# First stage of a fused attention and MLP layer: x transposed a unit ahead, V products in banks of their own, V weights summed by ScalarE, two weight pieces fetched ahead

## The chip, the cores and the metric

The kernel runs on one core of a Trainium2 chip. The metric is the device time of one execution in microseconds. Three runs of the kernel before gave a median of 1518.57 us (1517.03 to 1524.56). The profile is of a separate execution, which took 1515.59 us.

A core has five engines, each with a queue that it works through in order: TensorE (PE; its weight loads are listed as PEld), VectorE (DVE), ScalarE (ACT), GpSimd (POOL) and SyncE (SP), which issues all DMAs of this kernel. Engines wait for each other by semaphores. TensorE's clock is granted by a throttle: 1.00 is full speed.

## The reference

The input x has 2048 rows of 512. It is normalized over its columns; the result feeds an attention of 32 heads of 16 columns and, in parallel, an MLP of width 1792. Both are added to x:

```python
def _A_ref(x, wqkv, wo):                 # D = 512, H = 32, Dh = 16
    q, k, v = split_heads(x @ wqkv)
    p = softmax(einsum("bhqd,bhkd->bhqk", q, k) * Dh ** -0.5)
    return merge_heads(einsum("bhqk,bhkd->bhqd", p, v)) @ wo
def _B_ref(x, w1, b1, w2, b2):           # F = 1792, tanh gelu
    return gelu(x @ w1 + b1) @ w2 + b2
xn = _layernorm(x)
return x + _A_ref(xn, A_wqkv, A_wo) + _B_ref(xn, B_w1, B_b1, B_w2, B_b2)
```

`split_heads` and `merge_heads` stand for the reshapes and transposes of the original.

## The kernel before

**Number format.** Operands are scaled by powers of two and split into a high and a low float16 part, and a product is the sum of three (high-high, high-low, low-high). So each weight piece has first to be read once for its largest magnitude or the sum of its magnitudes; from that come the scales.

**Units.** Attention is worked off four heads and 512 queries at a time, in 16 units per such tile, 512 units in all. Of a unit, `s_half` makes the scores [q, k] that only serve the row maxima: 4 quarter products into one of three S banks, and one VectorE reduce (`mt`, L259); four of them to a unit. `s_end` turns the 16 units' maxima into one column (`mneg`, L270). 19 units later (LEAD), `e_half` makes the transposed scores (pT), ScalarE exponentiates them (`pe`), and `v_half` multiplies with V. What is left of TensorE goes to a fill: first V products, then projections of further heads, MLP, output projection. A fill group is 12 to 42 products.

**The first stage** (from L897) is what has to be there before units can start. x arrives in 16 row tiles of 128 (`load_x`); four of them are a block. `stats` normalizes a block, `transpose_x` turns one of its four column chunks with four TensorE transposes into a bank, copies it out as the high part (L816) and subtracts for the low part, on VectorE (L822) for chunks 0 and 2 and by a ScalarE copy `pf` and GpSimd (L819, L820) for chunks 1 and 3. `project` makes the query or key rows of four heads for one block (12 products of 128x512), writes them to DRAM (`stg`, L503, L504), and `stacks` reads them back in the order that the scores need (L403). Block 0 goes through first; then, for blocks 1, 2 and 3, a projection of keys and one of queries, and four first-tile units `tile_and_unit` (scores and maxima only), with 3 V products after each pair of score halves. Block 2 is transposed after its predecessor's four units, block 3 between units 4 to 7. `prep_v` measures the two halves of the V weights on VectorE (`am_v`, L742), makes their scale and splits them (L144, L145).

**Weight pieces.** 18 pieces of 512 KB (`chunk`, `fetch`, tile `wch`, three buffers, which the two V halves use first) are read in this stage for their magnitudes alone: seven of w1, seven of w2 and two of wo by a ScalarE sum (L850), and last two of the Q/K weights of further heads by VectorE (L742). `measure` hands them out, one or two after each unit; `fetch` issues the DMA of one piece ahead of the one in use. All these DMAs stand in SP's one queue with the x loads and the stacks. After the stage, `prepare` (L994 to L1000) reduces the sums and makes the scales; `rest` fills with the remaining V groups and the projections.

**What sets the order.** In the first stage TensorE's order is the program's (`manual_schedule`); the other engines' instructions are ordered by a list scheduler with its own costs, except those marked `keep_in_program_order`. From unit 16 on every queue is in program order. PSUM has eight banks: three S, three T, one D, one V. `vbank` goes round a list of tags (`free`): before, T, D, T, V, T for transposes, projections and V products alike. `NV` V groups of 12 products are made in the first stage, the others by the fill; units 16 to 18 take 36 products in bursts (`LFILL`).

The end is `last_one`: the last head group's output is normalized, transposed, split (L385 to L391) and multiplied with the last rows of wo; final adds are VectorE's (L1156).

Of the kernel before, what the change touches and what calls it, by code (L numbers as in the profile page):

```python
# [9 lines left out]
F32 = mybir.dt.float32  # L10
# [8 lines left out]
P = 128  # L19
S = 2048  # L20
D = 512
# [21 lines left out]
GELU_C = 0.7978845608028654  # L43
# [8 lines left out]
def layer_kernel(ctx: ExitStack, tc: tile.TileContext, x, wqkv, wo, w1, b1, w2, b2, out):  # L52
# [492 lines left out]
    def run(gen):  # L545
        for _ in gen:
            pass
# [169 lines left out]
    with ExitStack() as st1:  # L717
# [23 lines left out]
        def absmax(dst, v):  # L741
            nc.vector.tensor_reduce(dst, v, axis=AX.XY if len(v.shape) == 3 else AX.X, op=ALU.max,  # L742
                                    apply_absolute_value=True)
            given("dve", 600)
# [5 lines left out]
        every = [w1v[:, :, i * W:(i + 1) * W] for i in range(7)]  # L750
        every = every + [w2v[:, 2 * i:2 * i + 2, :] for i in range(7)] + [wov[:, 0:2, :], wov[:, 2:4, :]]
        wqk = wqkv[:, 0:2 * D].rearrange("(c p) (w n) -> p w c n", p=P, w=2)
        every = every + [wqk[:, w, :, W:2 * W] for w in range(2)] + every
        NM = 18
        amx = work.tile([P, 16], F32, name="amx")
        am_all = work.tile([P, 16], F32, name="am_all")
        fac1, inv1 = [], []

        def fetch(k):
            while len(loads) <= min(k + 1, NM + 15):  # L760
                loads.append(chunk(every[len(loads)]))
            return loads[k]

# [43 lines left out]
        def vbank():  # L807
            turn[0] += 1
            return banks(free[turn[0] % len(free)])
# [17 lines left out]
        def prep_v():  # L827
            am = work.tile([P, 3], F32, name="am_v")
            for i in range(2):
                absmax(am[:, i:i + 1], wvf[i])  # L830
                yield
            nc.vector.tensor_tensor(am[:, 2:3], am[:, 0:1], am[:, 1:2], op=ALU.max)
            box = []
            yield from scales(am[:, 2:3], 1, sbank, box)
            inv, fac = box
            fac_v.append(fac)
            for i in range(2):
                cs = slice(i * W, (i + 1) * W)
                split(wvh[0][:, :, cs], wvh[1][:, :, cs], wvf[i], inv[:, 0:1])

        def some(gen, n):
            for _ in range(n):
                next(gen, None)

        def measure():

            for n in range(16):
                v = fetch(n)
                dst = am_all[:, n:n + 1] if n < 7 else amx[:, n:n + 1]
                pin(nc.scalar.activation(v, v, AF.Abs, scale=1.0 / SPREAD, accum_out=dst))  # L850
                yield
            for w in range(2):
                v = fetch(16 + w)
                for m in (2, 3):
                    absmax(am_all[:, 8 + 2 * m + w:9 + 2 * m + w], v[:, :, (m - 2) * P:(m - 1) * P])
                yield
            for w in range(2):
                absmax(am_all[:, 10 + w:11 + w], wfs[1][w])
                yield

        ms = measure()

        def v_tiles():
            for t in range(NV):
                yield from whole(v_group(t, wvh, lambda: (vbank(), None)))

        vs = v_tiles()

        def tile_and_unit(t):

            for k in range(2):
                s_half(t, 2 * k)
                s_half(t, 2 * k + 1)
                some(vs, NV * 12 // 32)
            s_end(t)

        def weave(*gens):
# [39 lines left out]
            run(whole(project(0, w, 0, ready_w[0], lambda: (vbank(), None), True)))  # L917
        for w in (1, 0):
            stacks(0, w, [0])
        with tc.manual_schedule(engines={mybir.EngineType.PE}):  # L920
            free[:] = ["T", "D", "T", "V", "T"]
            for c in range(NC):
                transpose_x(1, c)
            some(pv, 2)
            for sb in range(1, NQB):
                ln = stats(sb + 1) if sb < 3 else iter(())
                for w in (1, 0):
                    pj = whole(project(0, w, sb, ready_w[0], lambda: (vbank(), None)))
                    for n in range(3):
                        some(pj, 4)  # L930
                        some(pv, 1)
                        if sb == 2:
                            some(ln, 3)
                    run(pj)
                run(pv)
                for w in (1, 0):
                    stacks(0, w, [sb])
                if sb == 1:
                    wfs.append(load_qk(1))
                if sb == 1:  # L940
                    clear(1)
                for j in range(4):
                    tile_and_unit(4 * sb - 4 + j)
                    some(ms, MEASURE[sb])
                    if sb == 1:
                        some(ln, 4)
                    elif sb == 2:
                        transpose_x(3, j)
                if sb == 1:
                    for c in range(NC):  # L950
                        transpose_x(2, c)
            for j in range(4):
                tile_and_unit(NT - 4 + j)
                some(ms, MEASURE[0])
            run(vs)
            run(ms)
        nc.sync.dma_start(b1_s, b1.rearrange("(f p) -> p f", p=P))
# [324 lines left out]
```

## Time and profile before

| | before |
|---|---|
| median of three runs | 1518.57 us |
| profiled execution | 1515.59 us |
| its span, first to last instruction | 1513.8 us |
| busy PE, DVE, ACT, POOL | 1476.7, 1384.8, 1257.5, 661.8 us |
| mean granted clock of TensorE | 0.993 |
| first transposed scores (pT), where the main stage begins | 117.60 us |
| last product with V of the main stage | about 1498.6 us |

A row of the order in time has the start, the length, the engine, the line, the operation, what it writes and reads, the count of merged instructions, and in brackets the idle time before it and who ended it. An instruction may be listed with its pipeline time, so neighbours overlap. Rows with SPq are DMA issues, and their length includes waits of the queue.

### The profile page before, as it was taken

To read this page: it belongs to the slowest core of one execution; us is meant where nothing else is said; L and a number is where in the kernel's file an instruction comes from. 1 tells how busy PE (TensorE), PEld (TensorE's weight loads), DVE (VectorE), ACT (ScalarE), POOL (GpSimd) and SP (SyncE) were. 2 spreads that over 40 slices of the span, in tenths; PEclk is the share of its full clock that TensorE was granted. 3 is DMA by queue.
4 is the path that set the end of the run, shared out by engine and by line. 5 is a ranking of instruction groups with operands and counts; after the bars stand their busy time and mean duration, and the time that the engine had idled before them with its cause. 6 is when DMAs were issued, how large, how long until landed. Compare 5 with 4: busy or idle time off the path is not lost.

```text
span 1513.8 us, 87872 instructions
## 1 busy us (share of the span) xinstructions
PE 1476.7 (98%) x39986; PEld 818.1 (54%) x39986; DVE 1384.8 (91%) x2317; ACT 1257.5 (83%) x2348; POOL 661.8 (44%) x686
## 2 busy tenths in 40 slices
PE   7889999999999999999999999999999999999998
PEld 3335555555555555555555555555555555555554
DVE  8679889999999999999999999999999999999933
ACT  5538878888899888899988889998888998888875
POOL 4101879522777511277831137772115787111110
PEclk9999999999999999999999999999999999999999
DMA  7451667314322311131111211132002210121432
GB/s 243 144 179 47 187 197 243 118 56 133 90 65 75 95 49 34 36 81 53 40 46 46 61 46 44 37 82 59 28 24 63 74 38 22 50 60 25 138 98 93
DMA packets 114413, 124.80 MB, mean 82 GB/s; under 512 B 24700, under 2 KB 86012, under 8 KB 114040
## 3 DMA queue, kind: packets, MB, share of 16 engines
q1 hardware_dynamic: 114040, 119.19, 26.6%
q8 instruction: 312, 5.11, 1.5%
q14 instruction: 61, 0.50, 0.1%
HBM read 81.66 MB, written 37.34 MB: 79 GB/s over the span
## 4 chain that ended last, share of the span: by engine, by line
PE 82%; DVE 9%; DMA 3%; issue 2%; SPq 1%; ACT 1%; POOL 1%; DVEq 0%; ACTq 0%; POOLq 0%
PE pV L168 24%; PE pD L168 22%; PE pT L168 17%; PE pS L168 17%; DVE mt L259 7%; PE pT L437 1%; DMA qk_d<-stg 1%; DMA wch<-in_B_w_dram 1%; DMA m_d<-mhl 1%; PE pD L437 1%; DMA wch<-in_A_wqkv_dram 0%; DMA wch<-in_A_wo_dram 0%; DMA xs<-in_A_x_dram 0%; ACT wch L850 0%; SPq L367 0%
## 5 line engine op out<-in xcount | busy, mean ns | idle before, releaser
L259 DVE TENSOR_REDUCE mt<-pS 128x1 f32<-128x512 f32 x2048 | 1306.9, 684 | 52.2 <-PE pS L168 31.7
L304 ACT ACTIVATE pe<-pT 128x512 f32<-128x512 f32 x2048 | 1111.7, 599 | 178.7 <-PE pT L168 74.6
L168 PE MATMUL pV<-pe,vv 64*32 64x512 f32 x8192 | 1075.2, 595 | 0.3 <-issue 0.2
L168 PE MATMUL pT<-qst,kst 64*32 64x512 f16 x8192 | 712.9, 377 | 6.4 <-DMA qst<-m_d 3.4
L168 PE MATMUL pS<-kst,qst 62*32 62x512 f16 x8192 | 622.4, 378 | 3.5 <-DVE mt L259 1.1
L168 PEld LDWEIGHTS <-qst 62*32 62x32 f16 x8192 | 280.5, 92 | 224.1 <-issue 56.9
L168 PEld LDWEIGHTS <-kst 64*32 64x32 f16 x8192 | 279.4, 91 | 175.1 <-issue 75.8
L168 PE MATMUL pD<-xb,wc 64*32 64x512 f16 x5376 | 360.8, 377 | 0.0
L168 PE MATMUL pD<-w_s,g 64*32 64x512 f16 x5376 | 359.2, 377 | 0.0
L168 PEld LDWEIGHTS pV<-pe,vv 64*32 64x32 f32 x8192 | 182.3, 105 | 90.2 <-issue 2.7
L168 PE MATMUL pD<-xt,wqk_h 64*32 64x512 f16 x2304 | 152.6, 378 | 1.0 <-issue 1.0
L168 PEld LDWEIGHTS <-wc 64*32 64x32 f16 x5376 | 116.8, 91 | 43.2 <-issue 1.1
L168 PEld LDWEIGHTS <-g 64*32 64x32 f16 x5376 | 113.1, 91 | 44.0
L360 POOL TENSOR_TENSOR osb<-osb,rb 128x512 f32<-128x512 f32 x31 | 39.8, 1284 | 203.8 <-DMA rb<-den_d 180.6
L1124 POOL TENSOR_TENSOR xa<-xa,yt 128x512 f32<-128x512 f32 x16 | 20.4, 1278 | 230.0 <-ACT yt L1122 200.8
L1079 POOL TENSOR_TENSOR t<-hh 128x512 f32<-128x512 f32 x56 | 58.2, 1040 | 69.4 <-ACT hh L1099 68.6
L1074 POOL TENSOR_TENSOR t<-t,hh 128x512 f32<-128x512 f32 x56 | 71.8, 1282 | 4.7
L1081 POOL TENSOR_TENSOR t<-t,hh 128x512 f32<-128x512 f32 x56 | 71.8, 1282 | 4.7
L1076 POOL TENSOR_TENSOR g<-t,g 128x512 f16<-128x512 f32 x56 | 65.1, 1163 | 4.7
L168 PEld LDWEIGHTS <-wqk_h 64*32 64x32 f16 x2304 | 53.3, 92 | 20.9 <-issue 3.4
L1073 POOL TENSOR_SCALAR t<-t,gs 128x512 f32<-128x512 f32 x56 | 38.8, 692 | 48.7 <-ACT t L1068 48.7
L168 PE MATMUL pD<-wo_s,oc 64*32 64x512 f16 x828 | 54.5, 378 | 0.0
(151 smaller groups left out, 863.7 us busy)
## 6 DMA issues: line engine op xcount, KB each, us to landing
wch<-in_B_w_dram SPq DMA_DIRECT2D x28, 512.0 KB
wc<-w_d SPq DMA_DIRECT2D x56, 256.0 KB
qk_d<-stg SPq DMA_DIRECT2D x32, 256.0 KB
rb<-den_d SPq DMA_DIRECT2D x124, 64.0 KB
w_d<-wsp SPq DMA_DIRECT2D x28, 256.0 KB
kst<-qk_d SPq DMA_DIRECT2D x128, 48.0 KB
qst<-qk_d SPq DMA_DIRECT2D x128, 48.0 KB
xs<-in_A_x_dram SPq DMA_DIRECT2D x16, 256.0 KB
```

The costliest lines, as they stand in the source:

```text
L168: p = nc.tensor.matmul(*args, **kw)
L259: nc.vector.reduce_max(mt_of[t][:, n, qt, kb:kb + 1], s, axis=AX.X)
L304: nc.scalar.activation(pe, st, AF.Exp, scale=scale_of[g // 2])
L360: pooled((1280, lambda: nc.gpsimd.tensor_tensor(osb, osb, rb, op=ALU.mult)), (620, lambda: nc.gpsimd.tensor_scalar(ot[:, 0], osb, 1.0, 0.0 ...
L437: nc.tensor.matmul(self.bank, lhs, rhs, start=start, stop=self.last and self.over())
L1073: pooled((690, lambda: nc.gpsimd.tensor_scalar(t1, t1, 1.0, gs[:, 1:2], op0=ALU.add, op1=ALU.mult)), (1280, lambda: nc.gpsimd.tensor_tenso ...
L1074: (1280, lambda: nc.gpsimd.tensor_tensor(t1, t1, hh, op=ALU.mult)),
L1076: (1160, lambda: nc.gpsimd.tensor_tensor(g[:, 1, f, :], t1, g[:, 0, f, :], op=ALU.subtract)),
L1079: pooled((1040, lambda: nc.gpsimd.tensor_tensor(t1, hh, hh, op=ALU.mult)), (620, lambda: nc.gpsimd.tensor_scalar(t1, t1, 1.0, 1.0 / GELU_A ...
L1081: (1280, lambda: nc.gpsimd.tensor_tensor(t1, t1, hh, op=ALU.mult)),
L1124: add = lambda: nc.gpsimd.tensor_tensor(xa, xa, yt, op=ALU.add)
```

## The change

- `transpose_x` of block 2 moves into unit 3 and behind it, that of block 3 into units 5 and 6, as an argument of `tile_and_unit`. Behind unit 3, 12 V products follow the transposes, ahead of projection 2.
- `free` is T alone from block 1 on, for transposes and projections; V groups take the D and the V bank in turn.
- The two V halves are summed by ScalarE, in program order, into a scratch tile.
- The two Q/K pieces become the first measured instead of the last, with the two maxima of the next heads' weights; `fetch` issues two pieces ahead in the first stage.
- Pieces are measured one after each unit and one after projections 2 and 3.
- `NV` is 8 instead of 9: one V group more is left to the fill.

Lines of the changed file are one lower than before up to L753 (`MEASURE` is gone).

```diff
-MEASURE = (2, 1, 1, 1)
-NV = 9
+NV = 8
...
-        every = every + [wqk[:, w, :, W:2 * W] for w in range(2)] + every
+        every = [wqk[:, w, :, W:2 * W] for w in range(2)] + every + every
...
-            while len(loads) <= min(k + 1, NM + 15):
+            while len(loads) <= min(k + (1 if pos[0] else 2), NM + 15):
...
         def prep_v():
-                absmax(am[:, i:i + 1], wvf[i])
+                junk = ph.tile([P, 4 * W], F32, name="wch", bufs=3)
+                tc.keep_in_program_order(nc.scalar.activation(junk.rearrange("p (a b) -> p a b", b=W), wvf[i], AF.Abs,
+                                                              scale=1.0 / SPREAD, accum_out=am[:, i:i + 1]))
...
         def measure():
+            for w in range(2):
+                v = fetch(w)
+                for m in (2, 3):
+                    absmax(am_all[:, 8 + 2 * m + w:9 + 2 * m + w], v[:, :, (m - 2) * P:(m - 1) * P])
+                absmax(am_all[:, 10 + w:11 + w], wfs[1][w])
+                yield
             for n in range(16):
-                v = fetch(n)
+                v = fetch(2 + n)
...
-                yield from whole(v_group(t, wvh, lambda: (vbank(), None)))
+                yield from whole(v_group(t, wvh, lambda t=t: (banks("DV"[t % 2]), None)))
...
-        def tile_and_unit(t):
+        def tile_and_unit(t, *chunks):
             for k in range(2):
                 s_half(t, 2 * k)
                 s_half(t, 2 * k + 1)
                 some(vs, NV * 12 // 32)
+                if chunks and chunks[k] is not None:
+                    transpose_x(t // 4 + 2, chunks[k])
...
+        some(pv, 2)
         with tc.manual_schedule(engines={mybir.EngineType.PE}):
-            free[:] = ["T", "D", "T", "V", "T"]
+            free[:] = ["T"]
+            some(pv, 1)
             for c in range(NC):
                 transpose_x(1, c)
...
+            for j in range(4):
+                tile_and_unit(j, [None, None, None, 0][j], [None, None, None, 1][j])
+                some(ms, 1)
+                some(ln, 8)
+            for sb in (2, 3):
+                if sb == 2:
+                    transpose_x(2, 2)
+                    some(vs, 3)
+                    transpose_x(2, 3)
+                    some(vs, 9)
+                    ln = stats(3)
...
+                some(ms, 1)
                 for j in range(4):
-                    tile_and_unit(4 * sb - 4 + j)
-                    some(ms, MEASURE[sb])
+                    t = 4 * sb - 4 + j
+                    if sb == 2:
+                        tile_and_unit(t, [None, 0, 2, None][j], [None, 1, 3, None][j])
+                    else:
+                        tile_and_unit(t)
+                    some(ms, 1)
```

More of the change, by code (lines that the diff above doesn't have):

```diff
@@ L930, in layer_kernel @@
                         some(pj, 4)
[L931 to L933 removed]
+                        some(ln, 3)
                     run(pj)
[L935 removed]
+                run(ln)
                 for w in (1, 0):
                     stacks(0, w, [sb])
[L938 to L941, printed above, removed]
+                some(ms, 1)
                 for j in range(4):
[L943 to L951 removed]
+                    t = 4 * sb - 4 + j
[4 more added lines that the diff above has]
+                    some(ms, 1)
             for j in range(4):
                 tile_and_unit(NT - 4 + j)
[L954 removed]
+                some(ms, 1)
             run(vs)
```

23 lines of the change are left out of this document (12 added, 11 removed).

## The prediction

> **What bounds the kernel now.** I read the shares of the page first, then busy time by stretches, then the order in time of each engine, and last the end.
>
> ```profile
> span 1513.8 us, 87872 instructions
> PE 1476.7 (98%) x39986; PEld 818.1 (54%) x39986; DVE 1384.8 (91%) x2317; ACT 1257.5 (83%) x2348; POOL 661.8 (44%) x686
> ```
>
> TensorE is busy for 98% of the span; 37 us are idle. Stretches of busy time (columns: length, busy of PE, PEld, DVE, ACT, POOL with instruction counts, granted clock, DMA share, GB/s) show where:
>
> ```profile
> 21.20:33.20 12.00, 9.64 (x43) 5.28 (x43) 10.65 (x34) 8.23 (x14) 2.31 (x2) 0.86 0.66 181
> 33.20:45.80 12.60, 11.41 (x105) 5.04 (x105) 12.60 (x20) 6.18 (x12) 1.54 (x1) 1.00 0.76 224
> 45.80:57.70 11.90, 8.30 (x24) 2.80 (x24) 5.56 (x18) 9.60 (x19) 2.31 (x2) 0.71 0.26 84
> 57.70:68.70 11.00, 11.00 (x105) 5.07 (x105) 10.10 (x17) 4.08 (x8) 2.31 (x2) 1.00 0.56 163
> 68.70:77.60 8.90, 5.67 (x34) 2.31 (x32) 1.63 (x3) 6.20 (x12) 1.15 (x1) 1.00 0.48 149
> 77.60:99.50 21.90, 21.90 (x198) 7.70 (x198) 19.22 (x32) 10.21 (x18) 1.16 (x1) 1.00 0.71 227
> 99.50:105.00 5.50, 1.03 (x12) 0.29 (x4) 2.80 (x6) 1.35 (x4) 0.00 (x0) 0.86 0.74 232
> 105.00:117.60 12.60, 12.49 (x83) 4.31 (x84) 8.25 (x18) 1.42 (x3) 0.00 (x0) 0.79 0.34 96
> 117.60:1498.60 1381.00, 1369.97 (x39225) 773.74 (x39224) 1289.43 (x2116) 1202.26 (x2249) 639.08 (x633) 1.00 0.25 72
> ```
>
> These are: x block 1 transposed and projected; tiles 0 to 3; x block 2 and its projection; tiles 4 to 7; projection 3; tiles 8 to 15 and a ninth V group; a wait; units 16 to 18, up to the first transposed scores (pT) at 117.60; the main stage; then the end. The change edits the first eight. What ended the waits (start, length, and in brackets the idle time before and its releaser):
>
> ```profile
> 23.43 1.16 PE L815 MATMUL pT<-ident,xs 128*128 128x128 f32 x4 [2.23 <-DVE xs L802]
> 34.98 9.65 DVE L259 TENSOR_REDUCE mt<-pS 128x1 f32<-128x512 f32 x16
> 45.54 1.06 ACT L850 ACTIVATE wch<-wch 128x1024 f32<-128x1024 f32 x1 [5.65 <-DMA wch<-in_B_w_dram]
> 50.95 6.82 PE L437 MATMUL pT<-xt,wqk_h 128*128 128x512 f16 x20 [1.14 <-POOL xt L820]
> 74.43 0.59 PE L437 MATMUL pT<-xt,wqk_h 128*128 128x512 f16 x2 [2.38 <-POOL xt L820]
> 96.46 2.75 PE L437 MATMUL pV<-wvh,xt 128*128 128x512 f16 x12
> 105.03 0.43 PE L277 MATMUL pS<-ident,mneg 64*32 64x64 f32 x4 [4.51 <-DVE mneg L270]
> 103.48 1.28 DVE L742 TENSOR_REDUCE am_all<-wch 128x1 f32<-128x512 f32 x2 [0.83 <-DMA wch<-in_A_wqkv_dram]
> ```
>
> At 45.54 ScalarE had stood 5.65 us before a weight piece; x's copies for projection 2 are queued behind it, so that projection ends at 57.7. A group of 12 products takes 2.75, so 24 take 5.5 at full clock. Between 99.5 and 105 VectorE waits for the last two pieces ahead of the row maxima (mneg). Tiles are VectorE's: 16 reduces in 9.65 us, 0.603 each, four to a tile.
>
> **The change, part by part.** I follow the changed kernel's own order on each queue and write times on the clock of the profile.
>
> *V sums on ScalarE, projection 1.* The rows that carry this part:
>
> ```profile
> 18.04 1.18 DVE L742 TENSOR_REDUCE am_v<-wch 128x1 f32<-128x1024 f32 x1
> 21.23 0.60 ACT L509 ACTIVATE stg<-pS 128x512 f16<-128x512 f32 x1 [0.46 <-PE pS L437]
> 22.87 1.34 ACT L800 ACTIVATE xs<-xs,sd 128x512 f32<-128x512 f32 x2 [1.04 <-DVE sd L794]
> 96.92 1.06 ACT L850 ACTIVATE wch<-wch 128x1024 f32<-128x1024 f32 x1
> 49.74 1.15 POOL L820 TENSOR_TENSOR xt<-pf,xt 128x512 f16<-128x512 f32 x1 [13.67 <-ACT pf L819]
> ```
>
> VectorE loses two reduces of a V half, 1.2 us each. ScalarE gains two sums like the one at 96.92, 1.15 each with the read-out. They stand behind the second projection copy (21.23, done by 21.8) and around two x scalings (1.34): 21.8 to 22.9, the scalings, 24.2 to 25.4. TensorE's order now puts the transpose of these sums ahead of x block 1, so block 1 starts at 25.9, not 23.43. All its transposes take the three T banks; the fourth waits for a copy (28.9). Piece 0, now a Q/K piece, is issued behind eight transfers of block 0, about 27.5, and VectorE stands before it, ahead of the scale of V and of x's third low part. The flight of a piece:
>
> ```profile
> 33.89 0.38 SPq L736 DMA_DIRECT2D wch<-in_B_w_dram  x1
> 38.19 1.06 ACT L850 ACTIVATE wch<-wch 128x1024 f32<-128x1024 f32 x1 [0.73 <-DMA wch<-in_B_w_dram]
> 98.10 5.36 DMA wch<-in_A_wqkv_dram
> 41.11 1.49 SPq L736 DMA_DIRECT2D wch<-in_B_w_dram  x3
> 83.94 7.03 SPq L736 DMA_DIRECT2D wch<-in_B_w_dram  x5
> ```
>
> 4.3 us alone, 5.4 among three. I take 4.3, since little else flies then: landing 31.8, two reduces 1.3, x's low part 33.8. The array is cold then, by these rows:
>
> ```profile
> 25.00:28.50 3.50, 3.50 (x15) 0.51 0.32 91
> 103.20:110.20 7.00, 5.09 (x27) 0.52 0.10 33
> ```
>
> After 2.2 us idle the clock was 0.51 in 25 to 28.5; after 4.5 us idle it was 0.52 until 5.2 us past the restart at 105.03. The changed kernel idles 4.7 us and then works in bits; a product at half clock takes 0.43. From 33.4 on it is busy: the clock is back near 38, 11 or so products at 0.43 and the rest at 0.23 end projection 1 at 39. Tile 0 starts at 39.5, not 34.98: **+4.5**. Bounds: +1.5 (piece 0 early, full clock, the later start alone) to +6 (a flight of 5.4).
>
> The Trainium skill, "TensorE: Matmul & The Clock Gate", section "What's actually happening", says that the array is halved after an idle window of about 3.4 us and freed after a busy one of that length. It speaks against this change, since the new gap of 4.7 us is longer than that and the old one was not; the trace halved the clock after 2.2 us already. By the rule the clock would be back at 36.8 instead of 38 and the sum 0.6 us lower.
>
> *x a unit ahead, projection 2.* Tiles 0 to 3 carry 16 reduces (9.65), two of piece 1 (1.3) and one low part (0.6): 39.5 to 51. Block 2's first two chunks are transposed in tile 3, the rest beside 12 V products that stood elsewhere (below). Pieces 3 to 5 go out behind block 1's stacks at 46 (41.11 before, later by the delay of projection 1) and land from 50.5. On ScalarE, piece 3 stands ahead of x's chunks 2 and 3: 50.5 to 51.6, copies to 53.2, GpSimd's low part 54.4. The V products cover TensorE until 53. Projection 2 goes on from there with about 0.2 us of wait and ends at **58.1**, 0.4 behind the 57.7 of before: the 6.4 us that the old one lost to ScalarE's wait and the cold clock pay for the late start. If the cover fails (piece 3 lands 3 us later), it costs these 3 and some 2.3 of cold clock.
>
> *Projection 3.* Block 3 is transposed in tiles 5 and 6, and no measured piece stands before its copies any more. Tiles 4 to 7 take 11.0 as before, the projection 5.5 instead of 8.9. It ends at 74.6: **3.0 ahead**. What is late next: ScalarE measures pieces 6, 7, 8 and 10 around the two evictions, which puts the query eviction at 78 and its stacks and pieces 11 to 17, queued behind on SP, at 84.0, no earlier than the 83.94 of before.
>
> *Tiles 8 to 15.* 32 reduces:
>
> ```profile
> 77.99 19.22 DVE L259 TENSOR_REDUCE mt<-pS 128x1 f32<-128x512 f32 x32 [1.55 <-PE pS L168]
> 98.73 1.06 ACT L850 ACTIVATE wch<-wch 128x1024 f32<-128x1024 f32 x1 [0.65 <-DMA wch<-in_A_wo_dram]
> 107.72 0.14 DVE L997 TENSOR_REDUCE am_all<-amx 128x1 f32<-128x2 f32 x1
> 111.50 0.41 PE L168 MATMUL pS<-kst,qst 62*32 62x512 f16 x8
> 117.60 0.60 PE L168 MATMUL pT<-qst,kst 64*32 64x512 f16 x8
> ```
>
> They end at 94.2. The ninth V group (2.75 at 96.46) isn't there, nor the wait for two pieces: mneg is ready at 95, **10 ahead** of 105.03.
>
> *Units 16 to 18.* Seven pieces are left behind SP's 83.94, as many as ScalarE measured then in the old kernel; its last began at 98.73, so the last ends near 99.9. VectorE's three small reduces for the scales stand there, ahead of the reduces of unit 17. TensorE has banks and V products until about 99.5. From the fourth S half of unit 17 to pT it needed 117.60 - 111.50 = 6.1; restarting at 101 it has pT at **107.1, 10.5 ahead**. With no wait (12.6 at a clock of 0.79 is 10.0 at full clock) it would be 105.0.
>
> *Own banks, pieces two ahead.* Tiles show no wait of TensorE for a bank, and SP's order, not the look-ahead, releases the pieces: nothing, from 0 to 1 us of gain where V products no longer share T.
>
> *Eight V groups.* The ninth moves to the main stage's fill, 12 products in half arrays. No unit is longer for it; the order of the end shows the remainder: 60 and 12 quarter-column products and six whole ones between the last transposes and the last output group, where 8 and 12 stood, and nine final adds on VectorE instead of six:
>
> ```profile
> 1505.90 0.68 DVE L391 TENSOR_TENSOR ot<-pS,ot 64x512 f16<-64x512 f32 x1 [1.46 <-ACT ot L390]
> 1506.51 0.73 DVE L1156 SCALAR_TENSOR_TENSOR ac<-pS,gs,ac 128x512 f32<-128x512 f32 x1
> 1507.16 3.37 DVE L1156 SCALAR_TENSOR_TENSOR ac<-pD,gs,ac 128x512 f32<-128x512 f32 x5
> ```
>
> Five adds take 3.37, so three more are **+2.0** after 1505.90; bounds 0 (they run while VectorE waits) and 2.75 (a whole group).
>
> *Sum:* -10.5 + 2.0 = -8.5 us. The profiled execution took 1515.59 us (span 1513.8 and 1.8 around it): 1507.1. The median of the runs shown, 1518.57, lies 3.0 above it, so I forecast 1510.1.
>
> **The rivals.** (a) ScalarE still holds x back: piece 3 lands at 53.5, projection 2 ends 5.3 later (3 and 2.3), the pieces behind it slide too: 1515.4. For it: the 5.65 us at 45.54; against: 12 V products as cover. (b) The pieces set the end: piece 10, ahead of the query eviction, comes 5 us later than the 76 of my count, and pieces 11 to 17, scales and pT with it: 1515.1. For it: the stage moved 227 GB/s from 77.6 to 99.5 and SP is one queue; against: flights here were 4.3 to 5.4. (c) The late start is bought cheaper (+1.5), and pieces and tiles follow 3 us sooner: 1507. (d) Slower: the fill, longer by three units, meets the attention's tile ends elsewhere, and ScalarE's evictions hold the exponentials in the main stage. It idles 11 us of 1381 now, over 512 units. From 8.5 / 512 = 17 ns more per unit on it is slower; 31 ns make that 0.5%, 1527. For it: VectorE 93% and ScalarE 87% busy there; against: instruction kinds and paces stay.
>
> **How the numbers follow.** About 0.5%, 7.6 us, is what a measurement can tell from no change: below 1511.0 is faster, above 1526.2 slower. My forecast 0.52 (its own range 1506 to 1514, 0.36 of the 0.52 below 1511.0), (a) 0.10, (b) 0.13, (c) 0.14, (d) 0.11, of which 0.09 past 1526.2. Faster 0.36 + 0.14 = 0.50; same 0.16 + 0.10 + 0.13 + 0.02 = 0.41; slower 0.09. The range, 1502 to 1520, leaves out (d) and what is under (c) with the end at nothing (1507 - 2 and tiles a little sooner).
>
> **What would show it.** Tile 0's first reduce near 39.5; no half clock in projections 2 and 3; no VectorE wait before mneg, which comes at 95; the scales' reduces waiting for ScalarE until about 100; first pT at 107; nine adds after the last split. It is wrong if ScalarE waits for a piece ahead of an x copy, if pT comes after 112, or if the time from pT to the last V product, 1381 before, changes by more than 3 us.

## The result, and the profile after

The changed kernel takes 1510.55 us in the median of 20 runs (1509.37 to 1518.92), the kernel before 1519.05 us in as many (1511.99 to 1526.89). The ratio is 0.9951, 95% interval 0.9938 to 0.9963, so the change makes it half a percent faster. The profiled execution took 1512.14 us.

First the page of the changed kernel, its span and its busy times:

```profile
span 1510.4 us, 87999 instructions
PE 1479.5 (98%) x40052; PEld 820.6 (54%) x40052; DVE 1385.1 (92%) x2317; ACT 1258.9 (83%) x2351; POOL 661.4 (44%) x685
```

Busy times say little, as before. The changed kernel by stretches (columns as in the prediction):

```profile
21.90:39.20 17.30, 12.34 (x52) 6.74 (x53) 13.07 (x35) 12.27 (x22) 2.32 (x2) 0.70 0.65 203
51.20:58.84 7.64, 7.64 (x38) 3.55 (x36) 5.57 (x16) 6.81 (x14) 2.33 (x2) 1.00 0.16 52
69.78:75.05 5.27, 5.27 (x25) 2.24 (x23) 1.08 (x3) 4.31 (x8) 0.00 (x0) 1.00 0.93 283
75.05:95.20 20.15, 18.60 (x175) 6.02 (x175) 20.06 (x34) 7.39 (x14) 1.16 (x1) 0.96 0.57 189
95.20:101.30 6.10, 5.63 (x40) 1.72 (x39) 2.65 (x9) 5.05 (x10) 0.00 (x0) 0.84 0.87 290
101.30:108.25 6.95, 6.08 (x48) 2.43 (x47) 5.40 (x10) 1.34 (x4) 0.00 (x0) 1.00 0.45 139
108.25:1496.05 1387.80, 1377.08 (x39325) 776.39 (x39324) 1290.59 (x2117) 1202.49 (x2249) 638.97 (x632) 1.00 0.25 72
```

Projections 2 and 3 run at full clock and TensorE is busy for all of their 7.64 and 5.27 us; projection 1 (first row) is slow, at 0.70. The rows of the order in time that answer to those of before:

```profile
26.64 0.37 PE L124 MATMUL pS<-ident,am_v 128*1 128x128 f32 x1 [5.09 <-DVE am_v L833]
30.86 0.69 DVE L741 TENSOR_REDUCE am_all<-wch 128x1 f32<-128x512 f32 x1 [1.12 <-DMA wch<-in_A_wqkv_dram]
39.24 1.29 DVE L258 TENSOR_REDUCE mt<-pS 128x1 f32<-128x512 f32 x2
53.57 5.34 PE L436 MATMUL pT<-xt,wqk_h 128*128 128x512 f16 x24
69.78 5.34 PE L436 MATMUL pT<-xt,wqk_h 128*128 128x512 f16 x24
77.05 1.06 ACT L857 ACTIVATE wch<-wch 128x1024 f32<-128x1024 f32 x1 [2.42 <-DMA wch<-in_B_w_dram]
95.24 0.20 DVE L269 TENSOR_REDUCE mneg<-mt 128x16 f32<-128x64 f32 x1
101.36 0.15 DVE L1012 TENSOR_REDUCE am_all<-amx 128x1 f32<-128x2 f32 x1 [2.51 <-ACT wch L857]
108.25 0.60 PE L167 MATMUL pT<-qst,kst 64*32 64x512 f16 x8
1499.69 0.68 DVE L390 TENSOR_TENSOR ot<-pS,ot 64x512 f16<-64x512 f32 x1 [1.46 <-ACT ot L389]
1500.87 1.54 DVE L1171 SCALAR_TENSOR_TENSOR ac<-pS,gs,ac 128x512 f32<-128x512 f32 x2 [0.49 <-PE pS L167]
1502.32 4.69 DVE L1171 SCALAR_TENSOR_TENSOR ac<-pD,gs,ac 128x512 f32<-128x512 f32 x7
```

Tile 0 starts at 39.24, mneg has nothing ahead of it at 95.24, the scales' last reduce waits for ScalarE until 101.36, the first pT comes at 108.25, and nine final adds stand at the end. The stage is 9.35 us shorter (117.60 to 108.25). From the last V product of the attention (which ends at 1496.05) to the end of the span it is 14.3 us, where it was 11.6: 2.7 lost. The last V products, before and after:

```profile
1501.65 0.61 PE L168 MATMUL pV<-pe,vv 64*32 64x512 f32 x4
1495.44 0.61 PE L167 MATMUL pV<-pe,vv 64*32 64x512 f32 x4
```

So in the kernel before the last one ends at 1502.26, not at about 1498.6 as the table ahead of the prediction has it, and from pT to it there were 1384.7 us, not 1381.

The stage and the end make -6.6. The rest, from pT to the last V product, is 3.1 us longer in this execution, and that is where the forecast had nothing. The prediction had named a change of more than 3 us there as a sign that it is wrong, and this sign did come, if barely. The order in time shows one large wait of TensorE there, at about 378 us, and what SP did ahead of it:

```profile
364.56 4.80 SPq L402 DMA_DIRECT2D kst<-qk_d  x8
369.41 4.76 SPq L402 DMA_DIRECT2D qst<-qk_d  x8
374.27 1.23 SPq L283 DMA_DIRECT2D m_d<-mhl  x2
376.73 1.15 SPq L288 DMA_DIRECT2D qst<-m_d  x4
378.43 0.65 PE L167 MATMUL pT<-qst,kst 64*32 64x512 f16 x8 [3.29 <-DMA qst<-m_d]
```

The stretches around it, with the granted clock in the column behind POOL:

```profile
375.00:378.40 3.40, 0.14 (x4) 0.00 (x0) 0.69 (x1) 0.26 (x1) 2.29 (x3) 0.81 0.05 12
378.40:380.40 2.00, 1.97 (x36) 0.94 (x42) 0.69 (x1) 1.09 (x2) 0.00 (x0) 0.50 0.54 172
380.40:382.40 2.00, 2.00 (x33) 1.01 (x28) 0.95 (x2) 0.74 (x2) 0.00 (x0) 0.50 0.36 91
382.40:384.40 2.00, 2.00 (x53) 1.37 (x41) 0.78 (x2) 0.63 (x2) 0.00 (x0) 0.62 0.56 149
```

The row maxima of tile 6 go through DRAM into the query stack (`m_d`, lines 283 and 288) before the next tile's transposed scores can start. Their store stands on SP behind 16 stack loads of the third head group, 9.6 us of issues. TensorE waits 3.29 us and then runs at half clock until about 383.9, 5.5 us, and loses half of that, 2.7 us: some 6 us in all, an estimate from these rows. The kernel before had a wait of 1.75 us there (at 389), without a half clock.

### The profile page after: what moved, and what is told of

It reads as the page before. It is cut to its first block, busy times and chain, and to the rows that moved or that the text cites. A ratio compares the mean times of both kernels' runs of the same rounds, so it can differ in the third digit from the quotient of the medians.

```text
span 1510.4 us, 87999 instructions
## 1 busy us (share of the span) xinstructions
PE 1479.5 (98%) x40052; PEld 820.6 (54%) x40052; DVE 1385.1 (92%) x2317; ACT 1258.9 (83%) x2351; POOL 661.4 (44%) x685
## 4 chain that ended last, share of the span: by engine, by line
PE 78%; DVE 9%; DMA 4%; POOL 4%; SPq 2%; issue 1%; ACT 1%; DVEq 0%; POOLq 0%; ACTq 0%
PE pV L167 23%; PE pD L167 21%; PE pT L167 17%; PE pS L167 16%; DVE mt L258 8%; POOL wsp L1005 1%; DMA wch<-in_B_w_dram 1%; DMA qk_d<-stg 1%; POOL wch L1003 1%; DMA m_d<-mhl 1%; DMA wq<-in_A_wqkv_dram 1%; POOL wsp L1004 1%; SPq L402 1%; PE pT L436 0%; POOL stg L518 0%
## 5 line engine op out<-in xcount | busy, mean ns | idle before, releaser
L258 DVE TENSOR_REDUCE mt<-pS 128x1 f32<-128x512 f32 x2048 | 1307.4, 684 | 50.2 <-PE pS L167 30.5
L167 PEld LDWEIGHTS <-wc 64*32 64x32 f16 x5376 | 117.6, 92 | 42.9 <-issue 0.6
L167 PEld LDWEIGHTS <-g 64*32 64x32 f16 x5376 | 113.3, 92 | 43.8
L167 PE MATMUL pD<-wo_s,oc 64*32 64x512 f16 x732 | 48.5, 378 | 0.0
```

Source lines behind the costliest of these rows:

```text
L167: p = nc.tensor.matmul(*args, **kw)
L258: nc.vector.reduce_max(mt_of[t][:, n, qt, kb:kb + 1], s, axis=AX.X)
```

## The experiments

All ratios are to the kernel before, run beside each kernel on the same chip. The table is put together from rows like those above: the first reduce of tile 0, the first mneg and the first pT, the time from the mneg of tile 6 to that of tile 7 (the stretch with the wait), and the time from the last V product to the end of the span, all in us of one profiled execution.

One execution is a small base. Up to about 360 us e9 is the same program as the changed kernel, e10 the same as e2, and e11 the same as the kernel before. Such twins differ by up to 1.3 us in tile 0, 2.6 in mneg and 1.7 in pT, so a smaller difference between two kernels in the table proves nothing by itself. The profiles of e1 and e10 are of the slowest of their runs (1527.57 and 1510.84 us).

| kernel | ratio (95% interval) | tile 0 | mneg | pT | tile 7 | end |
|---|---|---|---|---|---|---|
| before | 1 | 35.0 | 104.7 | 117.6 | 45.6 | 11.6 |
| changed | 0.9951 (0.9938 to 0.9963) | 39.2 | 95.2 | 108.2 | 49.3 | 14.3 |
| e1 before, eight V groups | 1.0021 (1.0002 to 1.0039) | 35.6 | 104.0 | 117.1 | 49.0 | 14.3 |
| e2 changed, nine V groups | 0.9911 (0.9884 to 0.9937) | 36.9 | 94.5 | 106.4 | 45.2 | 11.6 |
| e3 V sums on VectorE | 0.9941 (0.9910 to 0.9972) | 35.9 | 94.4 | 107.2 | 50.5 | 14.3 |
| e4 Q/K pieces last | 0.9987 (0.9971 to 1.0004) | 37.5 | 99.3 | 111.4 | 47.9 | 14.3 |
| e5 x transposed late | 0.9982 (0.9963 to 1.0000) | 38.1 | 100.6 | 111.0 | 50.2 | 14.3 |
| e6 dummies in the idle time | 0.9949 (0.9930 to 0.9967) | 36.1 | 93.2 | 108.7 | 49.3 | 14.3 |
| e8 old banks, one piece ahead | 0.9942 (0.9924 to 0.9959) | 36.0 | 92.0 | 105.2 | 49.2 | 14.3 |
| e9 changed, stacks apart | 0.9894 (0.9865 to 0.9924) | 37.9 | 93.9 | 106.6 | 43.1 | 14.3 |
| e10 nine groups, stacks apart | 0.9912 (0.9880 to 0.9943) | 38.0 | 97.0 | 107.7 | 43.8 | 14.2 |
| e11 before, stacks apart | 0.9982 (0.9964 to 1.0000) | 35.0 | 104.1 | 117.3 | 43.4 | 11.6 |
| e12 e9, pieces from ScalarE's queue | 0.9893 (0.9874 to 0.9912) | 36.7 | 93.2 | 105.6 | 43.1 | 14.3 |
| e13 e12, V sums on VectorE | 0.9919 (0.9901 to 0.9938) | 35.4 | 92.6 | 104.8 | 43.1 | 14.3 |

**e1 and e2: the ninth V group, taken from the old kernel and given back to the new one.**

```diff
-NV = 9          # e1, in the kernel before
+NV = 8
...
-NV = 8          # e2, in the changed kernel
+NV = 9
```

> The kernel before with eight V groups in the first stage instead of nine, nothing else. My theory: the ninth group (2.75 us) stood in the wait for the two Q/K pieces, so mneg stays at 105.0 and the first pT at 117.6 (within 0.5); the group then costs its remainder behind the last V product: from that product to the end of the span 14 instead of 11.5 us, nine final adds. Whole: 2 to 2.8 us slower than before. Rival: the fill takes the group up in idle time of TensorE: the end of the span comes 11.5 to 12.5 us after the last V product, whole within 1 us of before. Second rival: the group was on the path of the stage, and pT comes 2.75 earlier: whole unchanged.

> The changed kernel with the ninth V group back in the first stage. My theory: its 12 products fall partly into TensorE's waits around 101 (1.3 us before the scores of unit 17), so pT comes 0 to 2 us later than 108.25, and the end is 2.8 us shorter (11.5 instead of 14.35 us behind the last V product): whole 1 to 2.8 us faster than the changed kernel. Rival: pT comes the full 2.75 later and the gain at the end is eaten: whole within 0.5 us of the changed kernel.

Of e1 the first theory held: pT stays (117.1), the end costs 2.7 more, with nine adds, and the whole is 0.21% or 3.2 us slower (0.3 to 5.9 by the interval). Both rivals fall by the trace. But e2 is 6 us faster than the changed kernel (0.40% by the ratios), twice what I allowed at most. The table shows what I had not looked at: with eight groups tile 7 takes 47.9 to 50.5 us in each kernel whose stacks were left alone, with nine 45.2 and 45.6. In the trace of e2 the same place reads, first the order in time and then a stretch:

```profile
370.74 2.29 SPq L283 DMA_DIRECT2D m_d<-mhl  x2
374.21 1.15 SPq L288 DMA_DIRECT2D qst<-m_d  x4
375.81 0.43 PE L167 MATMUL pT<-qst,kst 64*32 64x512 f16 x8 [1.70 <-DMA qst<-m_d]
```

```profile
375.80:378.00 2.20, 2.19 (x64) 1.42 (x72) 1.10 (x2) 1.67 (x4) 1.55 (x2) 1.00 0.53 182
```

The wait is 1.70 instead of 3.29 us, and the clock stays at 1.00: the eight transposed scores take 0.43 us, where they took 0.65 behind the longer wait. One group of 12 products less in the fill starts the MLP, and with it the loading of the third head group's stacks, a little earlier against the tile's end. That was a new theory then, and e9 was made for it.

**e9, e10, e11: the stacks kept away from the end of a tile.** One condition more in `more_stacks`, in the changed kernel (e9), with nine groups too (e10), and in the kernel before (e11):

```diff
-        if g + 2 < NG and pos[0] - LEAD >= 64 * (g + 1) + 3:
+        if g + 2 < NG and pos[0] - LEAD >= 64 * (g + 1) + 3 and 3 <= pos[0] % 16 <= 12:
```

> The changed kernel, in which the stacks of the next heads are not issued in units 13 to 15 and 0 to 2 of a tile (the function more_stacks alone has one more condition); still eight V groups. My theory after the runs with eight and nine groups: with eight, the fill before the MLP ends one group later, so the first stacks of the third head group stand on SP ahead of the maxima's way through DRAM at the end of tile 6; TensorE then waits 2.5 to 4.2 us for the query stack at about 380 us and the clock is halved for some 5 us more (tile 7 takes 47.9 to 50.2 us, with nine groups 45.2 to 45.6). Without these stacks there, tile 7 takes 43 to 45 us, no half clock at 380, and the whole is 4 to 6 us faster than the changed kernel: 1504.5 to 1506.5. Rival: the wait is the way through DRAM itself (two transfers behind each other) and the stacks only stood by: the wait stays above 1.5 us, tile 7 above 45, whole within 2 us of the changed kernel.

> The changed kernel with nine V groups and the stacks kept away from the tile's end. My theory: the two gains add where they do not overlap. With nine groups the wait at 376 was 1.70 us without a half clock, so the stacks give 1 to 1.7 us: 1503 to 1504 against 1504.7 with nine groups alone, 6.5 to 7.5 us faster than the changed kernel. Rival: with nine groups the wait was of another cause, and the whole stays within 0.5 us of 1504.7; or the stacks put off collide with the next tile's transfers, and it is slower than 1506.

> The kernel before with the stacks of the next heads kept out of units 13 to 15 and 0 to 2 of a tile, nothing else. It tells what part of the changed kernel's loss at tile 7 the kernel before has too. My theory: with nine groups the wait for the query stack was 1.75 us at 389 without a half clock, so tile 7 takes 43.1 to 43.8 us instead of 45.6 and the whole is 1.5 to 2.5 us faster than before; the change itself is then worth some 13 us (1502.3 against 1515 to 1516). Rival: before's wide scatter comes from this place, a half clock in some executions and none in others; then the gain is 4 us or more and the scatter falls below 6 us.

e9 in the order in time, and a stretch behind it:

```profile
367.37 1.23 SPq L283 DMA_DIRECT2D m_d<-mhl  x2
369.82 1.16 SPq L288 DMA_DIRECT2D qst<-m_d  x4
```

```profile
368.00:374.00 6.00, 6.00 (x184) 3.35 (x176) 5.72 (x10) 5.04 (x10) 0.93 (x1) 1.00 0.25 69
```

The store goes out as soon as the maxima are split (the second split ends at 367.35) and TensorE does not stop. How long the store stands behind the second split at this place says the same for every kernel: 5.2 to 6.7 us in the seven with eight groups and the old condition, 2.8 in the two with nine, 0.03 in the five with the new condition. The waits of TensorE in the main stage, grouped by what ended them (sum, times, longest), first the row of the changed kernel, then the largest group of e9, where that wait is gone from the list:

```profile
PE pT L167 <- DMA qst<-m_d: 4.2, 3, 3.3
```

```profile
PE pD L167 <- issue: 1.9, 2, 1.4
```

Tile 7 takes 43.1 us, 6.2 less, and e9 has a median of 1502.32 us: 8.6 us below the changed kernel by the ratios. The collision is shown; the 2 us beyond it are within the intervals. The rival, that the way through DRAM itself is the wait, falls.

e11 gains 2.7 us (0.18%), of which tile 7 has 2.2, and still scatters over 12.7 us (1508.48 to 1521.23): the old kernel's scatter does not come from this place. So with the collision out of both, the change is worth 1514.76 - 1502.32 = 12.4 us of the medians, which are from two chips, and 0.88% or 13.4 us by the ratios. The two intervals, taken together, leave room for about 8 to 19.

e10 is a miss: 1506.25 us in the median, 3.9 above e9 on the same chip, where I expected the gains to add. Its ratio is that of e2 (0.9912 and 0.9911), and the intervals of all three overlap, so the runs don't tell whether the condition gains anything with nine groups. Its trace shows two losses, and nothing ties either of them to the condition. The end takes 14.2 us, as with eight groups, because TensorE's clock is halved there (0.50 from 1500 to 1505): the last 12 products take 5.30 us, and the final adds, six as in e2, wait for them. In e11, with nine groups and the same condition, these products take 2.76 us and the end 11.6.

```profile
1499.82 5.30 PE L436 MATMUL pD<-wo_l,ot 64*128 64x512 f16 x12
```

And tile 4, where e10 and e2 are still the same program, holds a wait of the same kind:

```profile
242.20 1.25 SPq L283 DMA_DIRECT2D m_d<-mhl  x2
247.21 1.18 SPq L288 DMA_DIRECT2D qst<-m_d  x4
248.86 0.62 PE L167 MATMUL pT<-qst,kst 64*32 64x512 f16 x8 [4.19 <-DMA qst<-m_d]
```

The second split ends at 238.23, so the store stood 4.0 us behind other issues on SP, a 512 KB weight piece among them; in e2 and e9 it goes out at once here. The reload came 3.8 us after the store's issue, at the upper end of what all kernels show at this tile (1.4 to 3.8). From the mneg of tile 0 to that of tile 4, e1 takes 193.2 us, e10 189.9 and e6 190.0 (part of it the wait for its pieces), the two other kernels with the old stage 187.8 and 188.6, the rest 181.4 to 186.7. The same program took 184.4 in e2 and 189.9 in e10, so much of this differs from one execution to the next. What decides it I did not separate; for many of those waits the profile names no releaser.

**e4: Q/K pieces last.**

```diff
-        every = [wqk[:, w, :, W:2 * W] for w in range(2)] + every + every
+        every = every + [wqk[:, w, :, W:2 * W] for w in range(2)] + every
...
         def measure():
+            for n in range(16):
+                v = fetch(n)
                 ...
             for w in range(2):
-                v = fetch(w)
+                v = fetch(16 + w)
```

> The changed kernel with the two Q/K pieces measured last again, by VectorE, and everything else as changed. My theory: the wait of 4.5 us ahead of mneg in the kernel before was that of VectorE, in whose queue the reduces of the last piece stand ahead of mneg. Then mneg comes at 100 to 102 instead of 95.2, TensorE waits there for 4 us or more and restarts at half clock, and pT comes at 111 to 114 instead of 108.25: whole 3 to 5.5 us slower than the changed kernel. Rival: the last of the 18 pieces sets the end of the stage whoever measures it, since the scales need all of them: pT stays within 1 us of 108.25. Both: projection 1 no longer has piece 0 in front of x's third low part on VectorE; tile 0 starts at 39.2 as now if that wait was covered (what I read in the trace of the changed kernel), 1 to 2 us earlier if it cost what I forecast.

The order in time of e4 on VectorE and TensorE:

```profile
95.14 1.28 DVE L741 TENSOR_REDUCE am_all<-wch 128x1 f32<-128x512 f32 x2 [5.69 <-DMA wch<-in_A_wqkv_dram]
99.32 0.21 DVE L269 TENSOR_REDUCE mneg<-mt 128x16 f32<-128x64 f32 x1
97.06 1.81 PE L167 MATMUL pS<-kst,qst 62*32 62x512 f16 x12 [7.17 <-DVE mt L258]
```

VectorE waits 5.69 us for a piece, TensorE 7.17 us behind it (the scores at 97.06 wait for banks that the reduces hold), mneg comes at 99.3 (expected 100 to 102) and pT at 111.4: 3.2 later. By the ratios the kernel is 0.36% slower, 5.5 us; what goes beyond the 3.2 is not placed. The rival had pT within 1 us and falls. Tile 0 at 37.5 lies in the span of the kernels with piece 0 on VectorE (36.7 to 39.2), so that wait costs nothing that can be seen.

**e5: x transposed late.**

```diff
-                tile_and_unit(j, [None, None, None, 0][j], [None, None, None, 1][j])
+                tile_and_unit(j)
...
-                    transpose_x(2, 2)
-                    some(vs, 3)
-                    transpose_x(2, 3)
-                    some(vs, 9)
+                    for c in range(NC):
+                        transpose_x(2, c)
...
+                    if sb == 2:
+                        transpose_x(3, j)
```

> The changed kernel with block 2 transposed only behind unit 3, directly ahead of projection 2, and block 3 a chunk after each of units 4 to 7, as before; the 12 V products behind unit 3 go back among the score halves. My theory: the transposes a unit ahead carry the gain of projections 2 and 3. Projection 2 then takes 8.9 to 11.9 us (the two old projections) instead of 7.6, projection 3 8.9 instead of 5.3, both with half clock; mneg comes at 100 to 103 instead of 95.2 and pT 5 to 7 us later: whole 5 to 7 us slower than the changed kernel. Rival: the pieces in SP's queue and on ScalarE set the end of the stage, not x: mneg comes later, but pT by less than 2 us, and the whole is within 2 us of the changed kernel.

In the order in time, and the stretch of projection 3:

```profile
55.99 3.18 PE L436 MATMUL pT<-xt,wqk_h 128*128 128x512 f16 x14 [1.04 <-POOL xt L819]
75.81 4.68 PE L436 MATMUL pT<-xt,wqk_h 128*128 128x512 f16 x14 [2.38 <-POOL xt L819]
```

```profile
70.10:80.50 10.40, 7.20 (x34) 2.71 (x32) 1.64 (x3) 6.07 (x12) 1.15 (x1) 0.84 0.62 198
```

Projection 3 takes 10.4 us instead of 5.3, with a wait of 2.38 us for GpSimd's low part and a clock of 0.84; projection 2 loses about 1.5 (it ends 21.1 us behind the start of tile 0 instead of 19.6) and, against the theory, has no half clock. mneg comes 5.4 later, as expected. pT comes only 2.8 later: from mneg to pT e5 takes 10.4 us, without a wait for pieces and at full clock, where the changed kernel takes 13.0 with its wait for the last pieces and its clock halved until about 97.2. The whole is 4.7 us slower by the ratios, between theory and rival.

**e6 and e3: the late start of projection 1.** e6 fills TensorE's idle time, e3 takes the V sums back to VectorE:

```diff
             free[:] = ["T"]
+            warm(20)    # e6: 20 products of zeros into a bank that is not read
...
-                junk = ph.tile([P, 4 * W], F32, name="wch", bufs=3)     # e3
-                tc.keep_in_program_order(nc.scalar.activation(...))
+                absmax(am[:, i:i + 1], wvf[i])
```

> The changed kernel with 20 dummy products of zeros (128x512, into a bank that nobody reads) on TensorE between the projection of block 0 and the transposes of block 1, where it idles 5 us. Nothing else changes. My theory: the half clock of projection 1 (0.50 from 26 to 34.5, 24 products in 7.5 us instead of 5.3) is the price of that idle time: with the dummies the clock stays at 1.00, projection 1 takes 5.3 to 5.7 us and tile 0 starts at 36.5 to 37.5 instead of 39.2; whole 0 to 2 us faster, less than 2 where the last pieces set the end of the stage. Rival: projection 1 is paced by what feeds it (copies and low parts of x, piece 0 on VectorE): tile 0 stays at 38.5 or later.

> The changed kernel with the two V halves summed on VectorE again, as before. My theory: the sums on ScalarE are what delays the transposes of x block 1 (26.6 in the changed kernel, 23.4 before), so here they start at 23.4 to 24.5, TensorE idles 2 to 3 us instead of 5, and tile 0 starts 2 to 3.5 us earlier than 39.2 (at 35.5 to 37). The rest of the stage follows by that much up to the wait for piece 10 on ScalarE, behind which the last pieces set the end: pT comes 0 to 3 us earlier, whole 0 to 3 us faster. Rival: VectorE, with two reduces of 1.2 us more and piece 0 in its queue ahead of the x copies, is late instead: tile 0 at 39 or later, whole within 1 us of the changed kernel or slower.

e6, order in time and stretches:

```profile
20.90 4.48 PE L890 MATMUL pV<-wvh 128*128 128x512 f16 x20
100.20 0.15 DVE L1013 TENSOR_REDUCE am_all<-amx 128x1 f32<-128x2 f32 x1 [2.46 <-ACT wch L857]
```

```profile
28.00:30.00 2.00, 1.89 (x11) 1.22 (x12) 0.81 (x3) 2.00 (x5) 1.16 (x1) 1.00 0.76 224
```

The clock stays full, tile 0 starts at 36.1 and mneg comes at 93.2, 2 us earlier. Not all of the 3.1 us at tile 0 is the clock: TensorE starts on block 1 at 25.5 here and at 26.6 in the changed kernel, and it does so at 25.5 in e9 too, without dummies. From that start to tile 0 it is 10.6 us here, 12.6 in the changed kernel and 12.5 in e9, so the half clock costs about 2 us. The scales still wait for ScalarE, until 100.20, and TensorE, which waits there too, runs at half clock again (0.59 and 0.56 in 102 to 106). So pT (108.7) gains nothing: whole unchanged. e3 does it the other way, tile 0 at 35.9 and pT 1.0 earlier, 1.5 us by the ratios, less than the interval can tell.

**e12 and e13: pieces 11 to 17 issued from ScalarE's queue.** Both stand on e9, e13 with the V sums on VectorE as well:

```diff
-                pin(nc.sync.dma_start(v, src))
+                pin((nc.scalar if len(loads) > 10 else nc.sync).dma_start(v, src))
```

> The kernel with the stacks apart, in which pieces 11 to 17 are issued from ScalarE's queue instead of SP's (so the list scheduler also puts the query eviction of projection 3 ahead of piece 10). My theory: what ends the stage is SP's one queue, in which pieces 11 to 17 stand behind the query stacks until 83 to 84, and the maxima's store behind the pieces. Here the pieces go out from 75 to 78 on, the last sum ends before 97 instead of 99.7 to 101.3, the scales' reduces wait for VectorE and no more for ScalarE, and pT comes at 103.5 to 105.5 instead of 106.6: whole 1 to 3 us faster than 1502.3. Rival: the transfers themselves are the limit (0.7 of the DMA engines in that stretch), or the pieces delay the stacks: pT stays at 106 or later, whole within 1 us or slower.

> The kernel before this one in the list (stacks apart, pieces 11 to 17 from ScalarE's queue) with the V halves summed on VectorE. The V sums on VectorE alone gave tile 0 at 35.9 instead of 39.2 and 1.6 us. My theory: with the pieces no longer at the end of the stage the earlier tiles come through to pT: mneg at 90 to 92.5, pT at 101 to 104, whole 1 to 2.5 us faster than the kernel before this one in the list. Rival: the pieces still end the stage, the start is worth nothing: within 0.5 us of it.

The order in time of e12:

```profile
93.16 0.20 DVE L269 TENSOR_REDUCE mneg<-mt 128x16 f32<-128x64 f32 x1
96.91 0.15 DVE L1012 TENSOR_REDUCE am_all<-amx 128x1 f32<-128x2 f32 x1
105.56 0.60 PE L167 MATMUL pT<-qst,kst 64*32 64x512 f16 x8
```

The scales' reduces no longer wait (96.91, no idle time before it), the last sum ends at 96.8 instead of 99.6. Yet pT comes at 105.56, only 1.0 earlier, less than twins differ by: units 16 to 18 take 12.4 us from mneg with no wait in them, since the clock is halved until about 97.7 (0.50 from 92 to 96). By the ratios e12 and e9 are equal (0.9893 and 0.9894); its median of 1499.98 us is the lowest of all. The 1 to 3 us that I expected are not shown. e13 has its pT 0.8 earlier and is 4.7 us slower than e12 on the same chip (1504.67). That refutes my theory for it. The two profiled executions differ by 1.9 us only, and tiles 1 to 4 have 2.3 of that (186.7 against 184.4); the rest of the 4.7 is in no profile, and the cause is open.

**e8: the two parts costed at nothing, undone.**

```diff
-            while len(loads) <= min(k + (1 if pos[0] else 2), NM + 15):
+            while len(loads) <= min(k + 1, NM + 15):
...
-                yield from whole(v_group(t, wvh, lambda t=t: (banks("DV"[t % 2]), None)))
+                yield from whole(v_group(t, wvh, lambda: (vbank(), None)))
...
-            free[:] = ["T"]
+            free[:] = ["T", "D", "T", "V", "T"]
```

> The changed kernel without the two parts that I costed at nothing: V products, transposes and projections share the T, D and V banks in one list as before, and pieces are fetched one ahead instead of two. My theory: neither stands on the path; 0 to 1 us slower than the changed kernel's 1510.6, pT within 1 us of 108.25. Rival: the look-ahead of two is what lets pieces 11 to 17 be issued together behind the query stacks; one ahead, each waits for the sum of the one before and a flight of 4 to 5 us, 7 pieces take 30 us or more, the last sum ends after 110 and pT comes at 115 or later: 7 us or more slower.

The rival falls (pT at 105.2), but pT is also 3 us earlier than the changed kernel's, where I had allowed 1. By the ratios, 0.9942 against 0.9951, the two parts are worth nothing that can be told, as I took; the median is 3.2 us lower, on another chip, so if anything they cost. In this execution tile 0 comes at 36.0 and everything follows 3 us sooner. Block 1 starts 1.1 us earlier here and the clock is back at about 30.9 instead of 35.8; kernels with the changed kernel's own start have tile 0 from 36.7 to 39.2, so I don't put that down to the banks.

## Why the prediction was right, and where it was not

The time was right to half a microsecond, 1510.1 against 1510.55, and the stage went by its steps. The sum was right in part because two errors cancel.

- **Projection 1, +4.5.** Measured +4.3 (39.24): the size was right, the make-up less so. TensorE's later start on block 1 has 3.2 of it (26.64 instead of 23.43; forecast 25.9, 2.5 later). Piece 0 landed at 30.9 and its wait, a term of the forecast, cost nothing that can be seen: without it, e4 takes the same 12.6 us from that start to tile 0. The half clock had a price: e2 and e12, in which it lasted 3.4 us, take 10.1 and 10.3, while the changed kernel and e4, e5, e9 and e10, in which it lasted 10.2 us, take 12.1 to 12.6. The Trainium skill, "TensorE: Matmul & The Clock Gate", "What's actually happening", adds that its window of 3.4 us runs freely, so that the moment of the change depends on where in it the work falls. The traces agree in part: in e2 the clock was back some 3 us after the same restart (26.84), in the changed kernel 9 us after it, which is more than two such windows. How long the half clock lasts thus differs between executions with the same order of this work: where TensorE starts on block 1 some 0.1 to 0.4 us after the clock falls (e2, e12) it is back 3.4 us after the fall, and where it starts 0.9 to 2.2 us after it (the other five) 10.2 us after. With the short half clock tile 0 comes at 36.7 to 36.9, so that the forecast of 39.5 met 39.2 is in part luck. The rows, e2 first:

```profile
30.00:32.00 2.00, 2.00 (x11) 1.15 (x11) 1.64 (x4) 2.00 (x5) 1.15 (x1) 0.96 0.44 98
```

```profile
34.00:36.00 2.00, 2.00 (x7) 0.74 (x6) 1.28 (x1) 0.25 (x1) 0.00 (x0) 0.56 0.93 332
```

- **Projections 2 and 3.** Ends forecast at 58.1 and 74.6, measured 58.84 and 75.05, without half clock and without a wait for a piece ahead of x (piece 3 does stand ahead of the copies of chunks 2 and 3, as forecast, but has landed). e5 shows that the transposes ahead carry this. Rival (a) did not happen.
- **Tiles 8 to 15.** mneg forecast at 95, measured 95.24; e4 gives the old wait back and loses 5.5 us. Rival (b) did not happen, though ScalarE did wait 2.42 us at 77.05 for a piece, the one before piece 10.
- **Units 16 to 18.** pT forecast at 107.1, measured 108.25: the last sum ended at 101.3, not 99.9. My bound of 105.0 without any wait counted 10.0 us from mneg at full clock; e5 and e10, at full clock, take 10.4 and 10.7. That e12 has pT at 105.56 is luck: its mneg is 2 us earlier and its clock halved for 4.5 us behind it. Of the changed kernel's 13.0 us, 2.6 are more than e5's; half of the 2.0 us at half clock (from mneg to about 97.2) makes 1.0, which leaves 1.6 for the wait for the pieces, an estimate.
- **Eight V groups, +2.0.** The term was mis-sized: the end costs 2.7, near the upper bound of 2.75, since VectorE also waits 0.49 us for products ahead of the first two adds.
- **"No unit is longer for it."** This step failed. The fill, one group longer, brings the third head group's stacks in front of the maxima's store at the end of tile 6: 3.7 us in tile 7 against the kernel before's profile, 6.2 against e9. It is rival (d) in kind, at one place and not per unit. The change of the fill moves DMAs, and I had not followed SP's queue past the first stage.
- **What cancels it.** The stage and the end give -6.6 in the profiles, and the collision takes 3.7 of it back, which leaves about 3; the runs show 7.4 by the ratio (5.6 to 9.4 by its interval). So the runs gained some 4 us more than these parts explain, and the forecast owes its closeness to that. With the collision out of both kernels (e11 to e9), pT is 10.7 earlier and the end 2.7 longer, and 5 us or so of the 13.4 are left. In these two profiles TensorE's idle time behind pT falls from 12.8 to 8.0 us, at several places between 171 and 360 us and at two near the end. The forecast had nothing there. But the twins differ by as much there (tiles 1 to 4 take 184.4 and 189.9 us in e2 and e10), and the intervals of e11 and e9 leave room for a gain of only 8, which the stage and the end would explain; whether the new stage is the cause is open.
- **Own banks, two ahead.** Nothing, within what can be told (e8).

The two profiled executions differ by 3.4 us of span where the medians differ by 8.5: the old one lay 3.5 us under its median, the new one 1.6 above. Only the repeated runs give the size.

## What to carry to other kernels

Work that is moved from one stage into a later fill also moves what starts when that fill ends: follow the queue of every DMA up to there, and look for a short round trip through DRAM that lands behind a long batch of loads. Where one in-order queue issues everything, keep batches away from the moments at which a chain of small transfers is on the path; one condition was worth as much in the changed kernel (8.6 us by the ratios) as the whole change. Where two kernels share a part word for word, compare their profiles there first: what differs in it is the scatter of one execution. Shortening a stage ahead of a wait gives nothing until that wait is gone (e6), and then only down to the next limit (e12).

## What was not expected of the hardware

An idle time of 3.29 us halved TensorE's clock for the next 5.5 us, one of 1.70 us at the same place did not: the longer wait cost 2.7 us beyond its own length. An idle time alone does not fix the price: in the first stage the half clock lasted 3.4 us in some executions and 10.2 in others of the same order of work. From tile 8 on, a tile takes the same to about 0.3 us in executions of different kernels with the same number of groups (tile 9 takes 42.84 to 42.95 us in all fourteen profiles), but for tile 10 (42.1 to 43.7) and the last (43.2 to 44.8). Tiles 1 to 4, where weight pieces and stacks share the DMA engines (0.53 of them busy up to 282 us in the changed kernel, 0.20 from 419 on), take 181.4 to 193.2. Most of what differs between these profiles behind pT, apart from tile 7, is made there.
